# A new order for all instructions of a fused attention and feed-forward kernel, without the zero matmuls that followed the first transposes

## The chip, the core and the metric

The kernel runs on one core of a Trainium2 chip. A core has five engines with instruction streams of their own: TensorE (PE, matmuls into the eight PSUM banks), VectorE (DVE), ScalarE (ACT), GpSimd (POOL, which here issues the converting loads) and SyncE (SP, which issues stores and transposing DMAs). The streams are joined by semaphores only, so each engine runs its instructions in the order in which they were written. The metric is the device time of one execution in microseconds, as the median of several runs.

## What is computed

Attention with a local window of 96 positions and 8 global ones, 4 batches of 768 positions, 8 heads of 64, with a linear bias by distance; then a feed-forward layer, 512 to 2048 to 512, with a squared ReLU. Cut to what matters:

```python
scores = scale * np.matmul(q, k.transpose(0, 1, 3, 2)) + bias
scores = np.where(is_global | is_local, scores, -1000000000.0)
a = np.exp(scores - np.max(scores, axis=-1, keepdims=True))
a = a / (np.sum(a, axis=-1, keepdims=True) + 1e-09)
x = np.matmul(a, v)        # then (batch, position) x (head, dim) = 3072 x 512
h = x @ w_in
r = np.maximum(h, 0.0)
out = (r * r) @ w_out
```

## The kernel before

The 3072 positions are 24 tiles of 128, six to a batch. Two tiles make one block of the feed-forward layer, so there are 12 blocks.

**Attention of a tile j.** GpSimd loads q, k and v and converts them to bf16 (`ld.q.1` and so on, later `load.6`). For the first eight tiles TensorE transposes q and k (`tr.0.j` for q, `tr.1.j` for k), and VectorE or ScalarE copies the result out of its bank (`T.0.j`, `T.1.j`); from tile 8 on a DMA of SyncE does this (`T.8`). Tile 0 is loaded in fp32 by SyncE (`plain`). `sc.j` are the scores: the tile's queries against its own keys and those of the tile before, in four banks (two for the first tile of a batch). For the first three tiles the bias is put into the banks by matmuls (`bias.j`); later it is multiplied in after the exponential (`mul.j.g`, with tables E and, for the first tile of a batch, E0). `exp.j.odd.g` runs on ScalarE; the name has the odd or even heads and then the half. `pv.j.half` multiplies with v; `norm.j.half` divides by the sum (a reciprocal and a product on VectorE). The keys and values of the eight global positions are copied over rows that are no longer needed: `gk.j` and `gv.j`, which may run on VectorE, ScalarE or GpSimd (`kl.j` is a copy of the keys in a buffer of its own). `trx.j` transposes the result on TensorE, and `xT.j` copies it out; from tile 8 on `xT.j` is a DMA.

**Feed-forward.** Blocks 0 and 1 multiply plainly: `s1.blk.s` for one of 8 slices of the hidden dimension, `relu.blk.s` out of the bank, `sq.blk.s` to square it. From block 2 on the first product, and from block 1 on the second, is done with seven products in place of eight: `xs`, `sum`, `isum` and `wsum` are the sums and differences of the operands (VectorE), `h.blk.g.p1` to `p7` and `s2.blk.p1` to `p7` the products (TensorE), `u` and `part` copies of intermediate results out of a bank, `c` the combination of such a copy with a bank and the ReLU (one custom VectorE instruction, or a plain ReLU for c21), `q` the square, `o` the combination into the output tile, `st` its store.

**What sets the order.** Every step is an operation of a plan, and the string `ORDER` lists all of them in the order in which they are written out. After a `:` stand the PSUM banks that the step takes, after `@` the engine (A, V, P) where there is a choice; `#2` is the second operation of a name. The instructions of one engine stand in the order of this list; what one step waits for follows from the data, the banks and the buffers. Loads queue on GpSimd in the list's order, and a `gv@P` stands in the same queue.

**The start.** Before the plan begins, line 372 runs eight matmuls of zeros into bank 7, while nothing has landed yet. In the plan, `warm:7` (line 532) is eight more of them, between the transposes of the first q tile and those of the first k tile.

Of the kernel before, what the change touches and what calls it, by code (L numbers as in the profile page):

```python
# [62 lines left out]
T.1.4@V xT.1@V pv.2.1:0 ld.k.5 ld.win.2.0 exp.3.1.1 gk.3@A ld.win.2.1 norm.2.0 s1.0.3:2 mul.3.0 s1.0.6:4 ld.win.4.0
tr.0.4:7 ld.q.5 ld.v.4 norm.2.1 mul.3.1 relu.0.6@A s1.0.3#2 gv.2@P pv.3.0:3 norm.3.0 trx.2:5 T.0.4@A pv.3.1:6
ld.win.1.0 norm.3.1 ld.win.0.1 xT.2@A sc.4.0:1047 exp.4.1.1 exp.4.1.0 tr.1.5:3 T.1.5@A s1.0.2:5 trx.3:6 xT.3@V
ld.win.0.0 ld.win.5.0 s1.0.2#2 s1.0.2#3 s1.0.2#4 relu.0.3@V exp.4.0.1 ld.v.5 gv.3@P exp.4.0.0 gk.4@V sq.0.6@V
relu.0.2@A s1.1.3:7 ld.win.7.0 relu.1.3@A load.6 s1.1.6:0 mul.4.1 tr.0.5:6 mul.4.0 sq.0.3@V s1.1.2:3 T.0.5@A ld.wout.3
pv.4.0:2 ld.wout.1 sq.0.2@V sc.5.0:4157 ld.wout.0 s1.0.4:6 relu.1.2@A exp.5.1.1 s1.0.1:3 sq.1.3@A exp.5.0.0 relu.0.4@V
s1.1.4:7 ld.wout.2 norm.4.0 pv.4.1:4 gv.4@P norm.4.1 sq.0.4@A load.7 exp.5.1.0 sq.1.2@A relu.1.4@A s1.0.0:6 gate.9
ld.wout.4 mul.5.0 s1.0.0#2 sq.1.4@A s1.0.0#3 s1.1.5:2 trx.4:1 exp.5.0.1 relu.1.6@V s1.1.1:4 ld.wout.5 s1.0.1#2  # L70
relu.1.1@A E0.1 mul.5.1 relu.1.5@A pv.5.0:7 s1.1.7:0 s1.1.0:5 sq.1.1@V norm.5.0 ld.wout.6 E0.0 sq.1.5@V tr.1.6:4
sq.1.6@A pv.5.1:2 relu.1.7@A tr.0.6:7 s1.0.0#4 norm.5.1 xT.4@A sq.1.7@A h.2.0.p2:0 ld.wout.7 T.1.6@V h.2.1.p2:1
trx.5:2 xT.5@V relu.1.0@A sq.1.0@A gate.14 h.2.0.p1:5 xs.2.0 s1.0.5:4 sum.1.2 s1.0.7:2 relu.0.1@A xs.2.1 gate.10
sum.1.0 sum.1.1 relu.0.0@A T.0.6@A sc.6.0:36 wsum.0.0 sum.1.3 sq.0.0@A sq.0.1@A s2.0.0.0:7 relu.0.7@A s2.0.1.0 load.9
exp.6.0.0 xs.2.2 s2.0.2.0 exp.6.1.0 s2.0.3.0 s2.0.0.1:2 s2.0.1.1 wsum.2.0 relu.0.5@A sq.0.7@A s2.0.2.1 load.8 mul.6.0
wsum.1.0 s2.0.3.1 tr.0.7:3 tr.1.7:6 gate.15 isum.0.0 h.2.1.p1:4 T.0.7@A s2.0.4.0 isum.0.1 s2.1.p1.0:3 isum.3.1 T.1.7@A
sq.0.5@A pv.6.0:6 isum.1.1 s2.0.4.1 s2.0.5.1 u.2.0.1@A c.2.0.c11 s2.0.5.0 gate.11 u.2.1.1@A h.2.1.p6 q.2.0.c11@A
isum.1.0 T.8 s2.0.6.1 u.2.1.2@A s2.0.6.0 isum.3.0 pv.6.1:0 h.2.0.p6 wsum.2.1 wsum.0.1 s2.1.p1.1 s2.0.7.1 c.2.1.c11
norm.6.0 gate.13 o.0.1@V st.0.1 s2.0.7.0 h.2.1.p7 part.1.p1@A s2.1.p6.0 u.2.0.2@A o.0.0@A u.2.1.3@A h.2.0.p7 h.2.1.p4
T.9 norm.6.1 wsum.3.0 u.2.0.3@A sc.7.0:1762 c.2.1.c21@A wsum.1.1 h.2.1.p5:0 c.2.1.c22 q.2.1.c11@A s2.1.p2.0:4  # L80
exp.7.1.0 exp.7.0.0 isum.2.1 load.10 h.2.0.p4 exp.7.0.1 mul.7.0 exp.7.1.1 s2.1.p2.1 isum.2.0 s2.2.p1.0:7 q.2.1.c21@A
mul.7.1 h.2.0.p5:1 s2.1.p6.1 part.1.p6@A trx.6:6 gate.12 c.2.0.c21@A load.12 pv.7.0:2 xT.6@A c.2.0.c22 q.2.1.c22@A
q.2.0.c22@A s2.2.p1.1 h.2.1.p3 s2.1.p7.0 wsum.3.1 o.1.p2 norm.7.0 h.2.0.p3 pv.7.1:5 s2.1.p7.1 q.2.0.c21@A st.0.0
c.2.1.c12 s2.1.p5.0 s2.1.p5.1 part.1.p7@A q.2.1.c12@A s2.1.p4.0 T.10 s2.1.p4.1 c.2.0.c12 gk.7@V q.2.0.c12@A o.1.p5
o.1.p4@A sc.8.0:6201 st.1.1 part.2.p1@A s2.1.p3.0 norm.7.1 sum.2.0 sum.2.1 s2.1.p3.1 trx.7:5 xT.7@V o.1.p3 h.3.0.p1:3
exp.8.1.0 gk.8@V h.3.1.p1:2 exp.8.0.0 exp.8.1.1 exp.8.0.1 h.3.0.p2:6 xs.3.0 u.3.1.1@A sc.9.0:1540 s2.2.p6.0 mul.8.0
xs.3.1 mul.8.1 u.3.0.1@A h.3.0.p6 exp.9.0.1 exp.9.1.1 gv.7@V h.3.1.p2:4 c.3.0.c11 h.3.1.p6 c.3.1.c11 exp.9.0.0
pv.8.0:0 s2.2.p6.1 pv.8.1:6 load.11 norm.8.0 u.3.1.2@A s2.2.p2.0:1 sum.2.2 gv.8@P q.3.1.c11@A norm.8.1 xT.8 h.3.1.p7
h.3.0.p5:4 u.3.0.2@A h.3.0.p7 s2.2.p2.1 exp.9.1.0 st.1.0 part.2.p6@A xs.3.2 u.3.1.3@A q.3.0.c11@A h.3.1.p5:0 s2.2.p7.0
u.3.0.3@A mul.9.1 mul.9.0 s2.2.p7.1 c.3.1.c22 T.12 c.3.0.c22 pv.9.0:6 h.3.1.p3 o.2.p2 h.3.0.p4 c.3.1.c12 load.15  # L90
norm.9.0 q.3.1.c22@A h.3.0.p3 s2.3.p1.0:5 s2.3.p1.1 c.3.0.c12 q.3.0.c22@A pv.9.1:0 c.3.0.c21@A part.2.p7@A norm.9.1
q.3.1.c12@A h.3.1.p4 q.3.0.c12@A h.4.0.p1:3 c.3.1.c21@A s2.2.p5.0 part.3.p1@A gk.9@V sc.10.0:6402 s2.2.p5.1
q.3.0.c21@A sum.3.0 sum.3.1 s2.2.p4.0 s2.2.p4.1 exp.10.1.0 sum.2.3 exp.10.0.0 exp.10.0.1 h.4.0.p2:4 T.11 u.4.0.1@A
exp.10.1.1 gk.10@V gv.9@A s2.3.p6.0 o.2.p5 mul.10.0 c.4.0.c11 xT.9 h.4.1.p1:6 o.2.p4@A mul.10.1 s2.2.p3.0 s2.2.p3.1
q.3.1.c21@A s2.3.p2.0:0 sum.3.2 u.4.1.1@A pv.10.0:2 pv.10.1:4 s2.3.p6.1 xs.4.0 gate.17 o.2.p3 part.3.p6@A xs.4.1
s2.3.p2.1 norm.10.0 h.4.0.p6 h.4.1.p6 q.4.0.c11@A gv.10@A norm.10.1 u.4.0.2@A load.13 s2.3.p7.0 sc.11.0:7124 u.4.1.2@A
sum.3.3 h.4.0.p7 h.4.1.p7 xs.4.2 exp.11.1.0 o.3.p2 exp.11.0.0 u.4.0.3@V s2.3.p7.1 sc.12.0:17 exp.11.1.1 exp.11.0.1
# [67 lines left out]
def kernel(  # L165
# [119 lines left out]
    HALVES = ((NBLK - 2, 0), (NBLK - 2, 1))  # L285
# [176 lines left out]
    for j in range(NT):  # L462
# [127 lines left out]
        def emit_sc(e, gs, j=j, todo=todo, open_sc=open_sc):  # L590
# [4 lines left out]
            if j >= NBIAS:  # L595
                open_sc(gs)
# [835 lines left out]
```

## Time and profile before

| | us |
|---|---|
| median of 3 runs | 198.78 |
| the runs | 198.13, 198.78, 200.09 |
| the profiled execution | 199.37 |
| its span, first to last instruction | 197.6 |

A stage by stage look at the profile: the first loads land between 3.9 and 9 us; attention of the first tiles alone fills 8 to 18 us; from 18 us on the products of the feed-forward part run among the attention of later tiles; after 190 us only the last block's output is left. In a row of busy time by stretch, a number such as 8.25 (x156) is the busy time in us and the number of instructions. In a row of the groups, the columns are busy time, mean duration in ns of one instruction, idle time of the engine just before them, and what ended it. Neighbouring instructions of VectorE and ScalarE overlap a little, so a mean duration is a few per cent more than what one adds to the engine's busy time. Matmul durations overlap widely: there the distance from start to start counts, which the chain of waits shows.

### The profile page before, as it was taken

What the parts mean: (1) busy time and instruction counts of PE and PEld (TensorE: products, weight loads), DVE (VectorE), ACT (ScalarE), POOL (GpSimd) and SP (SyncE); (2) the same over time, 40 slices, a digit from 0 to 9 for tenths busy, and PEclk for the clock granted to TensorE, in tenths of its full rate; (3) what the DMA queues carried; (4) which work ended last, traced back from release to release, by engine and by line L of the source; (5) the groups of instructions that cost most, each with busy time, mean ns of one, the idle gap of its engine ahead of it and who ended that gap; (6) DMA issues with size and microseconds to landing.
All of it is one profiled execution on the core that took longest, in us unless ns stands there. A gap on an engine that the chain in (4) does not pass through costs nothing.

```text
span 197.6 us, 6777 instructions
## 1 busy us (share of the span) xinstructions
PE 191.9 (97%) x2776; PEld 169.6 (86%) x2776; DVE 173.2 (88%) x423; ACT 163.0 (82%) x335; POOL 80.4 (41%) x101
## 2 busy tenths in 40 slices
PE   7989999999999999999999999999999999999993
PEld 3578999866989999899989999989899989999992
DVE  8159869999999999799999999999899999989872
ACT  6379989966999898999789998998989879774750
POOL 8999988586045309603192903080410001000000
PEclk9999999999999999999999999999999999999999
DMA  6999999999999999999999999999695711114023
GB/s 127 153 158 171 181 181 185 182 202 159 139 209 191 75 200 88 145 174 210 151 129 203 114 124 194 160 121 92 136 81 116 154 55 56 27 30 163 0 106 106
DMA packets 111857, 26.91 MB, mean 136 GB/s; under 512 B 103379, under 2 KB 109011, under 8 KB 111827
## 3 DMA queue, kind: packets, MB, share of 16 engines
q0 software_dynamic: 80256, 13.37, 91.8%
q1 hardware_dynamic: 31570, 13.11, 32.5%
q8 instruction: 21, 0.34, 0.6%
q14 instruction: 10, 0.07, 0.1%
HBM read 27.26 MB, written 6.29 MB: 170 GB/s over the span
## 4 chain that ended last, share of the span: by engine, by line
PE 95%; DVE 2%; issue 1%; ACT 0%; DVEq 0%
PE bank L1212 35%; PE bank L950 32%; PE bank L1061 7%; PE bank L599 6%; PE bank L748 5%; PE bank L1339 4%; PE bank L372 2%; PE bank L506 2%; PE bank L532 1%; DVE qkT L433 1%; PE bank L816 1%; PE bank L579 0%; ACT qkT L429 0%; DVE o L1287 0%; DVE v L433 0%
## 5 line engine op out<-in xcount | busy, mean ns | idle before, releaser
L1015 ACT ACTIVATE hs<-hr 128x512 bf16<-128x512 f32 x72 | 44.8, 641 | 5.1 <-DVE hr L995 4.7
L665 ACT ACTIVATE esc<-bank 128x512 bf16<-128x512 f32 x78 | 42.9, 614 | 1.3 <-PE bank L599 1.0
L1212 PE MATMUL bank<-wsum,hsum 128*128 128x256 bf16 x264 | 36.2, 273 | 0.0
L1212 PEld LDWEIGHTS <-hsum 128*128 128x128 bf16 x360 | 32.1, 98 | 4.1 <-issue 0.5
L995 DVE CUSTOM_DVE_ANT_0 hr<-bank,early 128x512 f32<-128x512 f32 x45 | 30.4, 685 | 2.5 <-PE bank L950 1.5
L950 PEld LDWEIGHTS <-win 128*128 128x128 bf16 x480 | 29.7, 98 | 1.0
L950 PEld LDWEIGHTS <-qk_first 128*128 128x128 bf16 x480 | 29.7, 98 | 1.0
L429 ACT COPY early<-bank 128x512 f32<-128x512 f32 x42 | 24.5, 591 | 3.6 <-PE bank L950 3.3
L690 DVE TENSOR_TENSOR at<-esc,E 128x1024 bf16<-128x1024 bf16 x39 | 26.7, 696 | 0.1
L1212 PEld LDWEIGHTS <-hs 128*128 128x128 bf16 x264 | 24.0, 98 | 2.6
L310 POOL DMA_DIRECT2D qk<-in_q_dram x18 | 16.0, 890 | 21.9 <-DMA qkT<-qk 20.6
L1212 PE MATMUL bank<-wout,hs 128*128 128x256 bf16 x176 | 24.9, 273 | 0.0
L310 POOL DMA_DIRECT2D v<-in_v_dram x18 | 16.0, 888 | 18.3 <-DVE v L480 14.9
L950 PE MATMUL bank<-xT,win 128*128 128x128 bf16 x320 | 23.4, 219 | 0.0
L431 POOL COPY v<-v 8x520 bf16<-8x520 bf16 x8 | 5.7, 718 | 43.3 <-PE bank L748 43.3
L950 PE MATMUL bank<-xs,qk_first 128*128 128x128 bf16 x320 | 22.8, 219 | 0.0
L779 DVE TENSOR_TENSOR x<-bank,rs 128x256 bf16<-128x256 f32 x48 | 20.4, 425 | 1.7
L865 ACT ACTIVATE hr<-bank 128x512 f32<-128x512 f32 x33 | 19.4, 598 | 1.3 <-PE bank L950 0.4
L748 PE MATMUL bank<-v,at 128*128 128x65 bf16 x352 | 17.8, 193 | 0.0
L1287 DVE TENSOR_TENSOR o<-bank,part 128x256 f32<-128x256 f32 (+2 forms) x34 | 13.8, 410 | 3.3 <-PE bank L1212 3.2
L429 ACT COPY part<-bank 128x256 f32<-128x256 f32 x29 | 10.9, 375 | 7.1 <-PE bank L1212 6.9
L310 POOL DMA_DIRECT2D qk<-in_k_dram x18 | 16.1, 897 | 0.9 <-DMA win<-in_moe_w_in_dram 0.5
(92 smaller groups left out, 367.0 us busy)
## 6 DMA issues: line engine op xcount, KB each, us to landing
out_dram<-o SPq DMA_DIRECT2D x22, 256.0 KB, 2.5
v<-in_v_dram POOLq DMA_DIRECT2D x24, 128.0 KB, 5.6
qk<-in_q_dram POOLq DMA_DIRECT2D x18, 128.0 KB, 5.0
qk<-in_k_dram POOLq DMA_DIRECT2D x18, 128.0 KB, 5.8
wout<-in_moe_w_out_dram POOLq DMA_DIRECT2D x8, 256.0 KB, 8.5
win<-in_moe_w_in_dram POOLq DMA_DIRECT2D x6, 256.0 KB, 6.9
qk_first<-in_k_dram POOLq DMA_DIRECT2D x5, 128.0 KB, 5.6
qk_first<-in_q_dram POOLq DMA_DIRECT2D x5, 128.0 KB, 5.7
```

The source lines that it names most:

```text
L310: nc.gpsimd.dma_start(out=dst, in_=src)
L429: nc.scalar.copy(dst, src)
L665: nc.scalar.activation(out=tiles[tag, j, g][:, odd], in_=tiles.pop(("sc", j, odd, g)).rearrange("p a c -> p (a c)"), func=Act.Exp, scale=s ...
L690: nc.vector.tensor_mul(at, tiles.pop(("esc", j, g)), bias)
L748: nc.tensor.matmul(out=po[:, hi, :], lhsT=tiles["at", j, g][:, odd, at * P : (at + 1) * P], rhs=v_sb[kj][:, h, :], start=(i == 0), stop=(i ...
L779: nc.vector.tensor_tensor(out=x[:, 4 * hf : 4 * hf + 4, :], in0=po[:, :, :D], in1=rs.to_broadcast([P, 4, D]), op=Alu.mult,)
L865: nc.scalar.activation(dst, src, Act.Relu)
L950: nc.tensor.matmul(out=tiles["h", blk, g, bank][:, n], lhsT=left_[:, s, k], rhs=right_[:, k], start=opens and n == 0 and k == 0, stop=k == ...
L995: nc.vector._custom_dve(TENSOR_ADD_SAT, out=hr, in0=src, in1=tiles.pop(("u", blk, g, i)), s0=float("inf"), s1=0.0,)
L1015: nc.scalar.activation(hs, hr, Act.Square)
L1061: nc.tensor.matmul(out=hT[:, c, cols], lhsT=w_in_sb[s][:, kt, c * P : (c + 1) * P], rhs=tiles["xT", blk][:, kt, cols], start=(kt == 0), st ...
L1212: nc.tensor.matmul(out=tiles["acc", blk, bank][:, cols], lhsT=left_[:, s], rhs=right_[:, cols], start=first and s == 0, stop=s == NSTEP - ...
```

## The change

It replaces `ORDER` by another list: every step is there as before except `warm`, but in another order, with other banks and in part other engines. Two lines of the table show the form (the first of each; the rest says nothing to a reader):

```diff
-tr.0.0:0 warm:7 tr.1.0:1 T.1.0@V bias.0.0:23 T.0.0@A sc.0.0 ld.win.3.0 exp.0.0.0 ld.k.1 tr.1.1:4 bias.1.0:5670 T.1.1@V ld.q.1
...
+ld.q.1 ld.k.1 ld.v.0 ld.k.2 ld.q.2 ld.q.3 ld.v.1 ld.k.3 ld.q.4 ld.k.4 ld.v.2 ld.q.5 ld.k.5 ld.v.3 ld.win.3.0
...
-    NKEEP = 8
...
-        if j == 0:
-            def emit_warm(e):
-                for _ in range(NKEEP):
-                    nc.tensor.matmul(out=psum(), lhsT=zero[:, :P], rhs=zero, start=True, stop=True)
-
-            plan.op(("warm",), {"PE": 0.216 * NKEEP}, emit_warm, key=base)
...
-        def open_sc(gs, j=j):
-            for n, (g, odd) in enumerate((g, odd) for g in gs for odd in range(2)):
+        def open_sc(gs, at=0, j=j):
+            for n, (g, odd) in enumerate(((g, odd) for g in gs for odd in range(2)), at):
...
-                deps.append(glob.get(("v", j - 1)))
+                deps += [glob.get(("v", j - 1)), land["v", j - 1]]
...
-    u_next = [0]
+    u_free = list(u_ring)
...
-                    u = u_ring[u_next[0] % NU]
-                    u_next[0] += 1
+                    u = u_free.pop(0)
...
+                        u = tiles.pop(("u", blk, g, i))
+                        nc.vector._custom_dve(TENSOR_ADD_SAT, out=hr, in0=src, in1=u, s0=float("inf"), s1=0.0)
+                        u_free.append(u)
...
-                for o, cols in zip(done, cuts):
+                for o, cols in zip([done[-1]] * len(cuts), cuts):
```

Besides the table: the zero matmuls of line 532 go (those of line 372 stay); a buffer of `u` is taken from a list of free ones instead of in turn; `pv.j` also depends on the landing of the v tile before; and in the last block the two parts of `o.11.p3` depend on both parts of the last product, so that the bank is read once all of it is written. Three places show what the table does.

ScalarE, up to the first results of the feed-forward part. The first rows are of before: `esc` are exponentials of the scores (tile 3 here), `qkT` copies of transposed q and k, `hr` the ReLU of the first product, `s1.0.6`.

```order
L665 ACTIVATE at_317<-bank_0_107 128x512
L665 ACTIVATE esc_379<-bank_4_111 128x512
L665 ACTIVATE esc_379<-bank_3_110 128x512
L665 ACTIVATE esc_390<-bank_6_113 128x512
L665 ACTIVATE esc_390<-bank_1_108 128x512
L429 COPY qkT_3_84<-qkT_0_81 128x4x8
L865 ACTIVATE hr_441<-bank_4_111 128x512
```

And of the changed kernel, up to the exponentials of tile 4 (`esc_456`, `esc_471`) and the copies `xT.1` (`xT_320`, out of bank 4, which `sc.5.0` takes next) and `xT.2` (`xT_486`):

```order
L429 COPY qkT_4_85<-bank_2_109 128x512
L660 ACTIVATE esc_414<-bank_6_113 128x512
L660 ACTIVATE esc_456<-bank_2_109 128x512
L660 ACTIVATE esc_456<-bank_1_108 128x512
L660 ACTIVATE esc_471<-bank_0_107 128x512
L429 COPY xT_320<-bank_4_111 128x4x128
L429 COPY xT_486<-bank_1_108 128x4x128
L660 ACTIVATE esc_471<-bank_7_114 128x512
```

Before, ScalarE turned to the feed-forward part after the exponentials of tile 3; now those of tile 4 come first, and there is no `hr` yet. In TensorE's stream the first `s1` step, `s1.0.3`, stands behind `sc.5.0` now, where it stood behind `pv.2.1`.

VectorE, at the first results of the feed-forward part, before (`hs` is the square of `hr`, `at` the product of `esc` with the bias table, `rs` and `x` a `norm`):

```order
L867 TENSOR_SCALAR hr_532<-bank_2_109 128x512
L433 COPY qkT_4_85<-qkT_0_81 128x4x8
L1100 TENSOR_TENSOR hs_539<-hr_441 128x512
L690 TENSOR_TENSOR at_565<-esc_500,E_101 128x1024
L690 TENSOR_TENSOR at_571<-esc_502,E_101 128x1024
L1100 TENSOR_TENSOR hs_539<-hr_532 128x512
L1100 TENSOR_TENSOR hs_539<-hr_541 128x512
L867 TENSOR_SCALAR hr_635<-bank_6_113 128x512
```

and in the changed kernel:

```order
L685 TENSOR_TENSOR at_545<-esc_456,E_101 128x1024
L862 TENSOR_SCALAR hr_569<-bank_5_112 128x512
L773 RECIPROCAL rs_572<-bank_7_114 128x4
L774 TENSOR_TENSOR x_571<-bank_7_114,rs_572 128x256
L773 RECIPROCAL rs_575<-bank_1_108 128x4
L774 TENSOR_TENSOR x_571<-bank_1_108,rs_575 128x256
L862 TENSOR_SCALAR hr_602<-bank_6_113 128x512
L433 COPY xT_610<-bank_5_112 128x4x128
L862 TENSOR_SCALAR hr_631<-bank_7_114 128x512
L433 COPY v_4_75<-v_0_71 8x8x65
```

The ReLU out of the bank moved to VectorE for more steps, the squares to ScalarE, and copies of global values (`v_4`) from GpSimd and ScalarE to VectorE.

VectorE at the very end. Before and after read alike there, apart from numbers; what differs is what the row before the last waits for. In both, the last two rows are the two parts of `o.11.p3`, which read the same bank:

```order
L1281 TENSOR_TENSOR o_4100<-bank_6_113,part_4032 128x256
L1161 TENSOR_TENSOR hsum_4052<-hs_3870,hsum_4052 128x512
L1281 TENSOR_TENSOR o_4127<-bank_6_113,part_4112 128x256
L1281 TENSOR_TENSOR o_4100<-bank_6_113,part_4098 128x192
L1281 TENSOR_TENSOR o_4100<-bank_6_113,part_4098 128x64
```

The part of 192 columns used to be read between the two halves of the last product; now TensorE writes all 256 columns first.

More of the change, by code (lines that the diff above doesn't have):

```diff
@@ L63 @@
[L63 to L97, printed above, removed]
```

180 lines of the change are left out of this document (107 added, 73 removed).

## Prediction

> **What bounds the kernel now.** I read the page's busy shares and the chain that ended last, then busy time by stretch, because a share over the whole span mixes a thin start with a dense middle.
>
> ```profile
> PE 191.9 (97%) x2776; PEld 169.6 (86%) x2776; DVE 173.2 (88%) x423; ACT 163.0 (82%) x335; POOL 80.4 (41%) x101
> PE 95%; DVE 2%; issue 1%; ACT 0%; DVEq 0%
> ```
> ```profile
> 8.50:18.10 9.60, 8.25 (x156) 6.88 (x154) 6.14 (x22) 6.93 (x15) 9.60 (x12) 1.00 2.29 161
> ...
> 31.00:190.00 159.00, 159.00 (x2357) 143.39 (x2355) 149.92 (x346) 138.79 (x285) 51.34 (x61) 1.00 1.18 131
> ```
> ```profile
> 18.10:190.00 171.90, 171.90 (x2558) 155.20 (x2555) 160.33 (x372) 150.48 (x308) 63.13 (x77) 1.00 1.23 135
> ```
>
> The columns after the stretch's length are PE, PEld, DVE, ACT, POOL (busy us and instructions), clock, DMA. From 18.1 to 190 us TensorE is busy for 171.9 of 171.9 us. It runs the same matmuls after the change, so nothing can be won in there; a new order can only keep it or open gaps. What can be won lies in the first 18 us, where TensorE also waits or runs matmuls that nobody reads, and in the tail. How that start goes is shown by the chain and the timeline:
>
> ```profile
> 1.19 3.60 PE bank L372 x8
> 4.79 0.85 PE bank L506 x4
> 5.64 2.41 PE bank L532 x8
> 8.05 0.45 PE bank L506 x4
> ...
> 9.28 0.40 PE bank L599 x8
> ...
> 10.00 0.87 PE bank L579 x8
> ...
> 11.62 0.62 PE bank L599 x16
> ...
> 15.09 0.36 PE bank L748 x8
> ...
> 19.61 0.22 PE bank L506 x4
> ```
> ```profile
> 18.12 1.49 PE L1061 MATMUL bank<-xT,win 128*128 128x128 bf16 x16
> ```
>
> L532 are the removed zero matmuls. L1061 at 18.12 is the first product of the feed-forward part, `s1.0.3`; from there on TensorE is dense. So I ask of the new order: when does `s1.0.3` start, and how much more of TensorE's work is then behind it?
>
> **The sum goes against the profiled execution**, 199.37 us (span 197.6 and 1.77 around it); the median of the three runs, 198.78, lies 0.59 lower, and the result is given on the median's scale.
>
> **Term A, the start.** Ahead of `s1.0.3` the new order puts three more transposed loads (`tr`), two more score sets (`sc.4`, `sc.5`), two more halves of `pv` and one more `trx`. By the chain's rows: 4 x 0.22 + 2 x 0.62 + 2 x about 0.3 (0.36 with its wait) = 2.7 us. If `s1.0.3` starts at 18.1 + 2.7 = 20.8 us, nothing is won or lost. Its start hangs on ScalarE: `sc.5.0` takes bank 4, and that is read last by the copy `xT.1`, behind 17 exponentials. The rows for these:
>
> ```profile
> L665 ACT ACTIVATE esc<-bank 128x512 bf16<-128x512 f32 x78 | 42.9, 614 | 1.3 <-PE bank L599 1.0
> L429 ACT COPY qkT<-bank 128x512 bf16<-128x512 bf16 x7 | 4.0, 590 | 1.5 <-PE bank L506 1.5
> L429 ACT COPY qkT<-qkT 128x32 bf16<-128x32 bf16 x4 | 1.0, 240 | 0.0
> ```
> ```profile
> plain<-in_q_dram SPq DMA_DIRECT2D x1, 256.0 KB, 3.1
> plain<-in_k_dram SPq DMA_DIRECT2D x1, 256.0 KB, 6.0
> ```
> ```profile
> 1.25 0.56 SPq L319 DMA_DIRECT2D plain<-in_k_dram  x1
> 1.34 0.89 POOL L307 DMA_DIRECT2D win<-in_moe_w_in_dram  x1 [0.17 <-issue]
> ```
> ```profile
> win<-in_moe_w_in_dram POOLq DMA_DIRECT2D x6, 256.0 KB, 6.9
> ...
> qk_first<-in_q_dram POOLq DMA_DIRECT2D x5, 128.0 KB, 5.7
> ```
>
> 17 x 0.55 (42.9/78) + 5 copies x 0.59 + 2 x 0.24 = 12.8 us. It can start when the first k tile is there: 1.25 + 6.0 = 7.25 us, then its transposes (0.45 at full clock): 7.75. So the removed 2.41 us buy little: the chain has the transposes behind them at 8.05, and they can't begin before 7.25. ScalarE then waits twice, for `sc.0.0` (0.40 and a hop) and for `bias.1.0`, `tr.1.1`, `sc.1.0` less the two exponentials beside them (0.87 + 0.22 + 0.62 - 1.1): 1.1 us. 7.75 + 12.8 + 1.1 = 21.65, and `sc.5.0` itself 0.62: `s1.0.3` at 22.3, 1.5 late. Without any such wait it is 21.2, 0.4 late. Neighbouring exponentials also start closer than 0.55 where none waits, so I take +0.8. The upper end, +2.5, has both waits and a further one just behind: `pv.4.0` stands after `gv.3` on VectorE (0.44) and `pv.4.1` after `mul.4.1` (0.70), with little between. The lower end, -0.9, is the case in which the k tile lands with the q tile (rival 1). The loads don't set this: `win.3.0`, issued first before (1.34), now follows 14 loads of q, k and v. GpSimd issued 12 instructions in the 9.60 us of its stretch, 0.80 each: 1.34 + 14 x 0.80 + 6.9 = 19.4, in time.
>
> **Term B, the clock.** The page grants 1.0 throughout, yet the weight loads of L532 show when full speed really came:
>
> ```profile
> 5.86 0.15 PEld L532 LDWEIGHTS <-early 128*128 128x128 bf16 x1 [0.28 <-issue]
> 6.29 0.15 PEld L532 LDWEIGHTS <-early 128*128 128x128 bf16 x1 [0.28 <-issue]
> 6.71 0.15 PEld L532 LDWEIGHTS <-early 128*128 128x128 bf16 x1 [0.28 <-issue]
> 7.03 0.53 PEld L532 LDWEIGHTS <-early 128*128 128x128 bf16 x3 [0.16 <-issue]
> ```
>
> One each 0.43 us until 6.71, then three in 0.53: twice the speed, after 5.7 us of unbroken work since 1.19. Without L532 the work breaks off after the first transposes (at 4.79 + 0.85 = 5.64) and resumes at 7.25. If TensorE is then still at half speed, the transposes take 0.85 in place of 0.45, and `bias.0.0` (half the columns of the L579 row, so 0.44) with `tr.0.1` (0.22), now hidden under a copy of 0.59, take 1.3 and show 0.7; `sc.0.0` 0.2 more: +1.3 on the way to the first exponential, and up to 0.9 more if `bias.1.0` (0.87) is slow too. Ends: 0, if the clock rises as before, and +2.2. I take +1.0, as the break of 1.6 us follows only 4.45 us of work, less than the 5.7 that it took before. [...]
>
> **Term C, VectorE.** The new order moves evictions to VectorE. Net counts from the two tables: `relu` +6, `c` +2, `q` +2, `sq` -4, `gv` +4 (two from ScalarE, two from GpSimd), `o` +3, and T, part, u, kl, gk, xT near zero together.
>
> ```profile
> L867 DVE TENSOR_SCALAR hr<-bank 128x512 f32<-128x512 f32 x3 | 2.1, 685 | 1.3 <-PE bank L1061 1.3
> L1100 DVE TENSOR_TENSOR hs<-hr 128x512 bf16<-128x512 f32 x5 | 3.3, 684 | 0.1
> L1017 DVE TENSOR_TENSOR hs<-hr 128x512 bf16<-128x512 f32 x8 | 5.5, 686 | 0.1
> L433 DVE COPY v<-v 8x520 bf16<-8x520 bf16 x4 | 1.8, 438 | 0.0
> L1287 DVE TENSOR_TENSOR o<-bank,part 128x256 f32<-128x256 f32 x32 | 13.2, 418 | 2.1 <-PE bank L1212 2.0
> L779 DVE TENSOR_TENSOR x<-bank,rs 128x256 bf16<-128x256 f32 x48 | 20.4, 425 | 1.7
> L778 DVE RECIPROCAL rs<-bank 128x4 f32<-128x4 f32 x48 | 8.4, 175 | 2.2 <-PE bank L748 2.1
> L690 DVE TENSOR_TENSOR at<-esc,E 128x1024 bf16<-128x1024 bf16 x39 | 26.7, 696 | 0.1
> L433 DVE COPY qkT<-bank 128x512 bf16<-128x512 bf16 x7 | 2.9, 418 | 1.9 <-PE bank L506 1.9
> ```
>
> 8 x 0.685 + 2 x 0.686 - 4 x 0.684 + 4 x 0.438 + 3 x 0.418 = 7.1 us. Against that, more of VectorE's work is done ahead of `s1.0.3`: seven norms (0.175 + 0.425), eight copies (0.418), two `mul` (0.696), two `gv` (0.438) and the f32 copy of the first tile (as the L867 row, 0.685) are 10.5 us, where the stretch 8.5 to 18.1 shows 6.14: 4.4 more. So the dense stretch has 160.3 + 7.1 - 4.4 = 163.0 us of VectorE in 171.9 - 2.7 = 169.2 us of TensorE, where before it had 160.3 in 171.9. VectorE's slack falls from 11.6 to 6.2 us. If it needed all its old slack TensorE would wait 5.4; if the slack was only waiting for TensorE, none. ScalarE, at 138.79 of 159, gets lighter. I take +0.7, near the lower end, as TensorE never waited at 94%.
>
> **Term D, the tail.**
>
> ```profile
> 194.16 0.36 DVE L1287 TENSOR_TENSOR o<-bank,part 128x192 f32<-128x192 f32 x1 [0.84 <-PE bank L1212]
> 194.57 0.28 PE L1212 MATMUL bank<-wout,hsum 128*128 128x64 bf16 x4 [0.45 <-DVE o L1287]
> 194.88 0.22 DVE L1287 TENSOR_TENSOR o<-bank,part 128x64 f32<-128x64 f32 x1 [0.37 <-PE bank L1212]
> ```
>
> The last four matmuls waited 0.45 for a read of their bank. Now they run first and both reads follow: the last read ends at about 194.85 in place of 195.10. The larger store is then issued some 0.1 later, just ahead of the last. I take -0.1, ends -0.5 and +0.2.
>
> Sum: 0.8 + 1.0 + 0.7 - 0.1 = +2.4; 199.37 + 2.4 = 201.8, on the median's scale **201.2 us**. The new code's other edits (which of the four `u` buffers is free, one more dependency of `pv` on a landed v tile, bank offsets) add no instruction; the v tile had been read by the tile before, so that wait is over.
>
> **The rivals.**
>
> 1. Faster: the k tile lands early. Its 6.0 us against 3.1 for the q tile come with a weight load of 256 KB that GpSimd issues 0.09 us later; now a load of 128 KB is issued there. If k lands by 5.6, the transposes follow each other without a gap, the clock rises as before, and ScalarE starts 1.65 us sooner: `s1.0.3` at 21.2 - 1.65 = 19.6 if it never waits, 20.65 if it waits as above, so at best 1.2 ahead of 20.8, and with the loads' 19.4 as a floor. With the tail, another 0.5 from exponentials that start closer, and no term C: 198.78 - 1.8 = 197.0. It decides if k lands before 6. Against it: a load is still issued in that place, and the next ones 0.8 apart. [...] Chance 0.16.
> 2. No change: the start loses about 0.8 to 1.0 by A or B, and the head start of VectorE and ScalarE on the attention lets every short wait of TensorE go: 198.8 to 199.6. For it: TensorE has been kept dense at 94% VectorE. Chance 0.19.
> 3. VectorE becomes the bound: its slack can't fall, TensorE waits 5.4, and with A, B and D 198.78 + 7.1 = 205.9. It decides where VectorE needs more than 96% of a stretch. For it: 163.0 of 169.2 is 96%. Against: 159 us at 94% without one wait. Chance 0.12.
>
> My own case has 0.53 and spans 199.8 to 203.5.
>
> **How the numbers follow.** About 1% (2 us) is what a measurement of this kernel can tell from no change: its three runs lie 1% apart. Below 196.8 is half of rival 1: 0.08. Within 196.8 to 200.8: the other half, rival 2, and 0.18 of my case: 0.45. Above: 0.35 of my case and rival 3: 0.47. The range 197.3 to 204.4 leaves out some 0.10 below and 0.07 above.
>
> **What would show it.** A: `s1.0.3` after 21 us, and ScalarE without a gap from the second score set to `xT.1`. B: the first transposes of the k tile 0.21 apart, not 0.11, and bias matmuls of 256 columns 0.21 apart. C: waits of TensorE for VectorE after 31 us, above 1 us in all. D: no wait of L1212 before the last four matmuls. I am wrong if `s1.0.3` starts before 20.5 with the middle still dense (then faster), or if the waits of TensorE after 31 us exceed 4 us.

## The result and the profile after

| | before | after |
|---|---|---|
| median of all runs, us | 199.31 (198.13 to 200.88, 20 runs) | 201.35 (199.45 to 202.83, 20 runs) |
| the profiled execution, us | 199.37 | 201.37 |
| its span, us | 197.6 | 199.6 |

The ratio of after to before is 1.0087, with a 95% interval of 1.0059 to 1.0114: slower by 0.9%, inside the range of the prediction and 0.15 us beside its number. The ratio leaves out three slow runs of after (202.5 to 202.8 us), so it stands for 1.7 us where the medians differ by 2.0. Against before the forecast was +2.4 us, so the close hit of the time itself owes something to before, whose median rose from 198.78 to 199.31 with more runs. The two profiled executions differ by 2.0 us, as the medians do, so they can be compared term by term. That comparison shows that the number was right for other reasons than those given.

The page after has the busy time of the engines and the shares of the chain that ended last:

```profile
PE 191.5 (96%) x2765; PEld 168.7 (85%) x2768; DVE 178.4 (89%) x435; ACT 158.6 (79%) x325; POOL 79.2 (40%) x99
PE 80%; DVE 6%; POOL 5%; ACT 3%; DMA 3%; issue 2%; DVEq 0%; POOLq 0%
```

TensorE's share of the chain fell from 95% to 80%, and two names are new in it: POOL and DMA. VectorE does 5.2 us more than before; 7.1 were reckoned. Busy time by stretch of after, with the columns as before:

```profile
8.50:20.55 12.05, 9.80 (x192) 7.60 (x190) 9.19 (x29) 11.04 (x24) 12.05 (x15) 1.00 2.16 160
20.55:190.00 169.45, 168.20 (x2470) 150.78 (x2470) 159.52 (x367) 140.68 (x286) 59.48 (x72) 1.00 1.23 134
31.00:190.00 159.00, 157.80 (x2328) 141.49 (x2329) 150.66 (x345) 132.35 (x270) 50.54 (x60) 1.00 1.19 131
```

The middle is no longer dense: 1.2 us of TensorE's 159.00 are idle, where none was. The start, in the timeline and in the row of DMA issues (median us from issue to landing last):

```profile
4.58 1.91 PE L506 MATMUL bank<-ident,plain 128*128 128x128 f32 x8
6.29 0.83 PE L573 MATMUL bank<-pb,early 128*128 128x128 bf16 x8
...
7.84 1.04 PE L573 MATMUL bank<-pb,early 128*128 128x256 bf16 x8
...
20.55 1.07 PE L1055 MATMUL bank<-xT,win 128*128 128x128 bf16 x16
```
```profile
plain<-in_k_dram SPq DMA_DIRECT2D x1, 256.0 KB, 3.9
```

The k tile landed 3.9 us after its issue, not 6.0, so the eight transposes follow each other without a gap. They stand 0.21 us apart, where before the transposes of k stood 0.11 apart (from 7.89 us on): half that speed. The granted clock rose to 1.0 at 6.7 us, and the bias matmuls of 256 columns behind that, eight in 1.04 us, stand 0.11 us apart. `s1.0.3` starts at 20.55, where 20.8 was the point at which nothing is won or lost.

The chain of waits of that stretch (start, length, what) says what held the start instead:

```profile
7.62 2.53 POOL qk_first L307 x3
10.16 5.68 DMA v<-in_v_dram
15.83 0.04 issue
15.88 0.42 PE bank L743 x8
```

GpSimd's issuing of loads, one behind the other, then the landing of the v tile of tile 2, then the `pv` that reads it. TensorE itself waited 0.33 us for that landing; from 16.3 us on the chain runs through VectorE, up to a copy that ends at 20.00. At 77 us stands the one large wait of the middle (idle time before the row, and its releaser, in brackets):

```profile
71.55 1.20 SPq L835 DMA_TRANSPOSE xT<-x  x1
77.18 0.43 DVE L917 TENSOR_TENSOR xs<-xT 128x512 bf16<-128x512 bf16 x1 [1.03 <-DMA xT<-x]
77.99 0.62 PE L945 MATMUL bank<-xs,qk_first 128*128 128x128 bf16 x8 [0.81 <-ACT hs L1009]
```

TensorE's row names ScalarE's `hs`, but `xs` is formed by VectorE at 77.18, and VectorE had been idle for 1.03 us until a transposing DMA landed. That is the true releaser. The tail:

```profile
195.16 1.06 PE L1206 MATMUL bank<-wout,hsum 128*128 128x192 bf16 x16
195.40 0.37 ACT L429 COPY o<-bank 128x256 f32<-128x256 f32 x1 [1.42 <-PE bank L1206]
196.25 0.49 DVE L1281 TENSOR_TENSOR o<-bank,part 128x192 f32<-128x192 f32 x2 [1.28 <-PE bank L1206]
```

The wait of 0.45 us is gone. From the start of the last product to the end of the span it is 199.6 - 195.16 = 4.4 us; before it was 197.6 - 193.18 = 4.4 as well.

### The profile page after: what moved, and what is told of

Same layout as the page of the kernel before. It is cut to its first block, busy times and chain, and to the rows that moved or that the text cites. A ratio compares the mean times of both kernels' runs of the same rounds, so it can differ in the third digit from the quotient of the medians.

```text
span 199.6 us, 6754 instructions
## 1 busy us (share of the span) xinstructions
PE 191.5 (96%) x2765; PEld 168.7 (85%) x2768; DVE 178.4 (89%) x435; ACT 158.6 (79%) x325; POOL 79.2 (40%) x99
## 4 chain that ended last, share of the span: by engine, by line
PE 80%; DVE 6%; POOL 5%; ACT 3%; DMA 3%; issue 2%; DVEq 0%; POOLq 0%
PE bank L1206 30%; PE bank L945 30%; PE bank L1055 7%; PE bank L743 4%; PE bank L594 4%; POOL qk_first L307 4%; PE bank L1333 3%; DMA v<-in_v_dram 3%; DVE at L685 2%; ACT hs L1009 1%; POOL v L307 1%; ACT esc L660 1%; DVE hr L990 1%; DVE x L774 1%; DVE hsum L1161 1%
## 5 line engine op out<-in xcount | busy, mean ns | idle before, releaser
L1009 ACT ACTIVATE hs<-hr 128x512 bf16<-128x512 f32 x70 | 43.4, 643 | 3.9 <-DVE hr L990 3.5
L660 ACT ACTIVATE esc<-bank 128x512 bf16<-128x512 f32 x78 | 43.6, 609 | 2.4 <-PE bank L594 2.2
L990 DVE CUSTOM_DVE_ANT_0 hr<-bank,early 128x512 f32<-128x512 f32 x46 | 31.3, 683 | 1.0 <-ACT hs L1009 0.4
L429 ACT COPY early<-bank 128x512 f32<-128x512 f32 x43 | 25.2, 593 | 8.5 <-PE bank L945 7.0
L1206 PE MATMUL bank<-wout,hs 128*128 128x256 bf16 x176 | 25.4, 273 | 0.0
L945 PE MATMUL bank<-xs,qk_first 128*128 128x128 bf16 x320 | 24.3, 219 | 0.9 <-ACT hs L1009 0.8
L310 POOL DMA_DIRECT2D v<-in_v_dram x18 | 16.3, 904 | 14.4 <-DVE v L480 9.2
L860 ACT ACTIVATE hr<-bank 128x512 f32<-128x512 f32 x25 | 14.9, 602 | 3.4 <-PE bank L945 2.4
L743 PEld LDWEIGHTS <-at 128*128 128x128 bf16 x352 | 15.1, 98 | 2.7 <-DVE at L685 1.4
L1055 PE MATMUL bank<-xT,win 128*128 128x256 bf16 (+1 forms) x160 | 15.9, 251 | 0.1
```

Of the source, the lines that this page charges most:

```text
L310: nc.gpsimd.dma_start(out=dst, in_=src)
L429: nc.scalar.copy(dst, src)
L660: nc.scalar.activation(out=tiles[tag, j, g][:, odd], in_=tiles.pop(("sc", j, odd, g)).rearrange("p a c -> p (a c)"), func=Act.Exp, scale=s ...
L743: nc.tensor.matmul(out=po[:, hi, :], lhsT=tiles["at", j, g][:, odd, at * P : (at + 1) * P], rhs=v_sb[kj][:, h, :], start=(i == 0), stop=(i ...
L860: nc.scalar.activation(dst, src, Act.Relu)
L945: nc.tensor.matmul(out=tiles["h", blk, g, bank][:, n], lhsT=left_[:, s, k], rhs=right_[:, k], start=opens and n == 0 and k == 0, stop=k == ...
```

## The experiments

All ratios are to the kernel before, with 95% intervals, five rounds each. For several runs a table gives the *lead* of TensorE: the start of a matmul in the reference kernel less the start of the same matmul in the run, in us, worked out from the two traces by matching TensorE's matmuls in order. A lead that stays level is kept; where it drops, something else than TensorE's own work came last. Each lead comes from one profile of each kernel. How far such profiles differ by themselves is seen from e6, e7, e9, e10 and e11, which run the same instructions as the changed kernel up to 77 us: `s1.0.3` starts at 20.54, 20.94, 19.65, 20.53 and 19.65 there.

**e1: before without the zeros.**

```diff
-tr.0.0:0 warm:7 tr.1.0:1
+tr.0.0:0 tr.1.0:1
```

> The kernel before without the eight zero matmuls of its plan (they feed no result); everything else as it was, the 256 KB weight load still first on GpSimd. Theory 1 (term B of the prediction, the clock falls back in the gap): the k tile lands at about 7.2 us as before, TensorE is idle from 5.6 to 7.2, and its transposes, the bias matmuls and the first scores then run at half speed (transposes 0.21 us apart): ratio to before 1.000 to 1.010. Theory 2 (the clock rises about 7 us after the start whatever stands in the gap, as the trace after the change suggests, where no gap arose): transposes 0.11 apart or 0.21 only for the first ones, the chain starts some 0.3 us earlier, ratio 0.995 to 1.000.

Ratio 1.0027 (0.9996 to 1.0057): no difference that can be told. It lies in theory 1's range, but theory 1's premise, a gap up to 7.2 us, did not occur: with the 256 KB weight load still first, the k tile landed 4.2 us after its issue, at 5.47.

**e2: before with the q tile loaded first.**

```diff
-ld.win.3.0 exp.0.0.0 ld.k.1 tr.1.1:4 bias.1.0:5670 T.1.1@V ld.q.1
+ld.q.1 exp.0.0.0 ld.k.1 tr.1.1:4 bias.1.0:5670 T.1.1@V
...
-ld.q.2 tr.0.2:3
+ld.q.2 ld.win.3.0 tr.0.2:3
```

> The kernel before with one load moved: the 128 KB q tile is issued first on GpSimd, the 256 KB piece of the weights that stood there comes after the q tile 2 load. Zeros stay. Theory (rival 1's mechanism: the first load of GpSimd decides when the k tile of SyncE lands): k lands 3.9 to 4.2 us after its issue in place of 6.0. The zeros keep TensorE until 8.05, so the time stays: ratio 0.997 to 1.003. Rival (the k tile lands early in the changed kernel for another reason): k lands 5.5 to 6.0 us after its issue, same ratio.

Ratio 0.9991 (0.9959 to 1.0022). k landed after 4.0 us, which looks like the theory, but e1 had 4.2 without the edit. So the first load of GpSimd does not decide it.

**e3: both.**

> The kernel before with both: the q tile first on GpSimd, and no zero matmuls. Theory 1 (the start is worth what rival 1 said, and the changed kernel lost it again by its own order between 10 and 20 us): the second score set comes about 2 us sooner, the first product of the feed-forward part at 16.3 to 17.0 us in place of 18.1, ratio 0.988 to 0.995, so faster than both kernels. Theory 2 (the lead is lost on later landings and on ScalarE in any order, as in the changed kernel): the first product of the feed-forward part at 17.5 to 18.2, ratio 0.997 to 1.002.

Ratio 1.0009 (0.9983 to 1.0035), although `s1.0.3` started at 16.09, 2.0 us sooner than before and sooner than theory 1 had it. TensorE still waits 0.9 us for copies of VectorE (1.1 before). The largest of its other waits are for loads and, at 90 us, for a transposing DMA:

```profile
11.10 0.40 PE L506 MATMUL bank<-ident,qk_first 128*128 128x128 bf16 x4 [0.78 <-DMA qk_first<-in_k_dram]
...
14.49 0.40 PE L506 MATMUL bank<-ident,qk_first 128*128 128x128 bf16 x4 [0.31 <-DMA qk_first<-in_k_dram]
...
89.99 0.23 PE L593 MATMUL bank<-qkT 64*128 64x128 bf16 x2 [0.68 <-DMA qkT<-qk]
```

**e12: e3 with two more loads reordered.**

```diff
-ld.q.2 ld.win.3.0 tr.0.2:3 norm.0.0 ld.k.2 T.0.2@V ld.k.3
+ld.q.2 tr.0.2:3 norm.0.0 ld.k.2 T.0.2@V ld.k.3 ld.win.3.0
...
-ld.win.6.0 sc.3.0:4361 ld.q.4 norm.1.1 ld.v.3
+ld.v.3 ld.win.6.0 sc.3.0:4361 ld.q.4 norm.1.1
```

> The kernel before without the zero matmuls and with the 128 KB q tile first on GpSimd, as in the run e3, and two more loads reordered: the first 256 KB piece of the weights now follows the k tiles 2 and 3, and the v tile 3 comes ahead of the second piece. Theory 1 (the landing of k, k and v tiles ends TensorE's waits of 0.78, 0.31 and 0.39 us at 10 to 19 us in the run e3, so the order of loads sets the start, and a lead is then kept by the order before, whose middle hardly waits): TensorE is 1.6 to 2.4 us ahead of the kernel before at 30 us (1.1 in e3), ratio 0.990 to 0.996, faster than both kernels. Rival (transposing DMAs and loads take the lead back between 80 and 110 us, as 0.96 us of e3's were): the lead at 30 us is there, but under 0.6 us is left at 110 us; ratio 0.997 to 1.002.

Ratio 1.0017 (0.9993 to 1.0041). Theory 1 fell, even in its first half: the waits for the k tiles 2 and 3 went, and three others stood up for what had been moved back. The ratio lies in the rival's range, but by luck, as the lead that the rival expected at 30 us was not there either (0.21).

```profile
13.82 0.40 PE L742 MATMUL bank<-v,at 128*128 128x65 bf16 x8 [1.22 <-DMA v<-in_v_dram]
15.43 0.40 PE L506 MATMUL bank<-ident,qk_first 128*128 128x128 bf16 x4 [0.46 <-DMA qk_first<-in_k_dram]
18.47 1.05 PE L1055 MATMUL bank<-xT,win 128*128 128x256 bf16 x8 [0.82 <-DMA win<-in_moe_w_in_dram]
```

TensorE's lead over the kernel before, at times of that kernel:

| us | 9.3 | 17.4 | 21.5 | 29.5 | 41.7 | 78 | 98 | 110 | 191 |
|---|---|---|---|---|---|---|---|---|---|
| e1 no zeros | 1.97 | 1.32 | 1.21 | 1.13 | 0.19 | 0.44 | 0.44 | -0.09 | -0.09 |
| e2 q first | 0.62 | 0.57 | 0.78 | 0.73 | 0.55 | 0.60 | 0.60 | 0.60 | 0.60 |
| e3 both | 2.50 | 1.83 | 1.15 | 1.09 | 0.91 | 1.13 | 0.39 | 0.17 | 0.17 |
| e12 loads | 2.49 | 0.89 | 0.21 | 0.21 | 0.25 | 0.27 | 0.13 | -0.86 | -0.86 |

Two things take most of a lead of 2 us. Up to 35 us it is the loads (in e1 one of these waits, 0.34 us, stands at 33.9): GpSimd issues one each 0.87 us, and in e1, e3 and e12 alike some tile came late. After 80 us it is transposing DMAs (`qkT<-qk` at 90 in e3, `xT<-x` ahead of the drop between 98 and 110 in e1 and e3).

**e4: after with the weight load first.**

```diff
-ld.q.1 ld.k.1 ld.v.0 ld.k.2 ld.q.2 ld.q.3 ld.v.1 ld.k.3 ld.q.4 ld.k.4 ld.v.2 ld.q.5 ld.k.5 ld.v.3 ld.win.3.0
+ld.win.3.0 ld.q.1 ld.k.1 ld.v.0 ld.k.2 ld.q.2 ld.q.3 ld.v.1 ld.k.3 ld.q.4 ld.k.4 ld.v.2 ld.q.5 ld.k.5 ld.v.3
```

> The changed kernel with the 256 KB piece of the weights first on GpSimd again, as before the change. Theory 1 (the prediction's own case hung on the k tile landing at 7.25; with this it happens): k lands at 7.0 to 7.3 us, the transposes of the k tile stand behind a gap, the first product of the feed-forward part starts at 21.5 to 22.5 us in place of 20.55, ratio to the kernel before 1.014 to 1.020. Theory 2 (the waits between 12 and 20 us come from other things and absorb the late start): it starts at 20.5 to 21.0, ratio 1.007 to 1.011.

Ratio 1.0180 (1.0148 to 1.0213), `s1.0.3` at 22.30: theory 1's numbers by another cause. k landed at 5.10. But every other load came later, and TensorE waited for the first of them:

```profile
8.17 0.40 PE L506 MATMUL bank<-ident,qk_first 128*128 128x128 bf16 x4 [1.45 <-DMA qk_first<-in_q_dram]
8.50 0.40 PE L594 MATMUL bank<-qkT 64*128 64x128 bf16 x8
9.02 0.40 PE L506 MATMUL bank<-ident,qk_first 128*128 128x128 bf16 x4
9.25 1.04 PE L573 MATMUL bank<-pb,early 128*128 128x256 bf16 x8
```

The matmuls behind this gap of 1.45 us ran at full speed (eight of 256 columns in 1.04 us). It is nearly as long as the gap that term B had (1.6 us), but it stands elsewhere: the granted clock had risen at 5.9 us, ahead of it, while term B's gap was to come before the rise.

**e5: after with the zeros put back.**

```diff
-T.0.0@V tr.1.0:1
+T.0.0@V warm:7 tr.1.0:1
```

> The changed kernel with the eight zero matmuls put back between the transposes of the first q and k tile. Theory 1 (the start is held by the loads, which GpSimd issues 0.87 us apart, and by what follows them, so that most of a lead or a lag of TensorE at 6 us is gone at 20 us): the first product of the feed-forward part starts at 20.6 to 21.6 us (20.55 without zeros), ratio to the kernel before 1.009 to 1.014. Rival (the chain from TensorE through ScalarE sets it, as terms A and B of the prediction had it): 22.0 to 22.6 us, ratio 1.016 to 1.020.

Ratio 1.0190 (1.0146 to 1.0233), `s1.0.3` at 21.40, later than in any of the six profiles that share the order without zeros. By its place the first theory, by its time the rival; in the profiled execution (span 200.8) the end came 1.2 us later than in the changed kernel. So the two don't agree on the size. In this order zeros cost something between 1.2 and 2 us, in the order before they cost nothing.

**e6: after with the tail as before.**

```diff
-s2.11.p3.0#2 s2.11.p3.1#2 o.11.p3 st.11.0#2
+s2.11.p3.0#2 o.11.p3 s2.11.p3.1#2 st.11.0#2
...
-                for o, cols in zip([done[-1]] * len(cuts), cuts):
+                for o, cols in zip(done, cuts):
```

> The changed kernel with the tail as before: the 192 columns are read between the two halves of the last product, and stored in that place. From the start of the last product to the end of the span it was 4.42 us before and 4.44 after. Theory (term D is nothing: the 0.54 us wait is traded against reads and stores that start later): 4.38 to 4.46 us, ratio to before 1.007 to 1.010. Rival (the later reads and stores cost, and the wait was hidden by the stores): 3.9 to 4.2 us, ratio 1.004 to 1.007.

Ratio 1.0097 (1.0064 to 1.0131), and from the start of the last product (195.48) to the end of the span (199.9) 4.4 us: the tail edit is worth nothing either way.

**e8: after with a table built later.**

```diff
-xT.0@V E0.1 sc.2.0
+xT.0@V sc.2.0
...
-mul.5.0 E0.0 T.0.6@V
+mul.5.0 E0.0 E0.1 T.0.6@V
```

> The changed kernel with one table for the first tile of a batch (a copy and a maximum, 0.9 us on VectorE) built at 28 us, where VectorE stood idle for 0.86 us, in place of 12.5 us, ahead of a norm and of the copy for which TensorE waits 0.93 us at 13.4. Theory 1 (VectorE's order costs in the start, the share of term C that lies ahead of the dense stretch): the wait at 13.4 falls to 0.1 to 0.4 us and the first product of the feed-forward part starts 0.3 to 0.7 us sooner (19.9 to 20.25), ratio to before 1.005 to 1.007. Rival (the landing of a v tile at 15.8 us holds the rest): the wait moves to 15.3 us, the first product starts at 20.4 to 20.6, ratio 1.008 to 1.010.

Ratio 1.0091 (1.0054 to 1.0129): the rival, one tile further on than I had it. The wait at 13.4 fell from 0.93 to 0.42, TensorE was 0.97 us ahead of the changed kernel at 16.3, and then the v tile of tile 3 landed 6.2 us after its issue at 12.75, that is at 18.9. In the changed kernel, which issues its loads in the same order, it landed at 18.0:

```profile
v<-in_v_dram POOLq DMA_DIRECT2D x1, 128.0 KB, 6.2
```
```profile
19.03 0.40 PE L743 MATMUL bank<-v,at 128*128 128x65 bf16 x8 [1.46 <-DVE qkT L433]
```

The `pv` of this row reads that tile, so it could not start before 18.9; the copy of VectorE that the row names ended 0.1 us after the landing. The lead at 21.3 us was -0.07. How late this tile lands differs between executions of one order, so the trace shows what took the lead in this execution. For all ten the ratio shows only that no gain was left.

**e7 and e9: the wait at 77 us.** Both put other work ahead of it on VectorE and TensorE; e9's edit (e7 leaves `o.2.p3` where it was):

```diff
-gv.10@V xs.4.0 xs.4.1 h.4.1.p6 o.2.p3
+gv.10@V norm.10.1 o.2.p3 xs.4.0 xs.4.1 s2.3.p2.1 sc.11.0:4276 h.4.1.p6
```

> The changed kernel with three steps moved ahead of the place where TensorE waited 0.81 us at 77 us (VectorE waits there for the transposing DMA of tile 9 before it can form xs of block 4): a norm of tile 10 on VectorE, and on TensorE the second half of a product of block 3 and the scores of tile 11 (some 0.9 us of work). Theory 1 (this wait is on the path that sets the end): the wait falls below 0.3 us, ratio to before 1.003 to 1.006. Rival (the next transposing DMA or VectorE takes it back at 90 to 110 us): the wait goes, and a wait of 0.4 us or more stands later that was not there; ratio 1.007 to 1.010.

> The changed kernel with the place at 77 us rearranged: VectorE does the second norm of tile 10 and reads the last bank of block 2 before it waits for the transposing DMA of tile 9, and TensorE does half a product of block 3 and the scores of tile 11 (0.9 us of work) before the product that needs xs of block 4. Theory 1 (the wait of 0.81 us for that DMA is on the path that sets the end): it falls below 0.3 us and TensorE is 0.5 to 0.9 us ahead of the changed kernel after it, ratio to before 1.003 to 1.006. Rival (the next transposing DMA, at about 93 us, takes it back): the lead is gone again before 110 us, with a wait of 0.4 us or more that was not there; ratio 1.007 to 1.010.

In e7 the scores of tile 11 overwrite two banks before block 2's last output is read from them, so part of the output is wrong; its ratio was 1.0138 (1.0107 to 1.0168). e9 had 1.0144 (1.0111 to 1.0177): not faster than the changed kernel, and by intervals that just touch slower. The wait itself went: TensorE's lead over the changed kernel rose from 0.86 to 1.85 us by 82 (the 0.86 it had from the start, ahead of the edit). It was taken back at the next places, and by more than the rival said: 1.13 at 87, 0.07 at 97, -0.70 at 107. One of these is the next block's transposing DMA:

```profile
91.98 0.43 DVE L917 TENSOR_TENSOR xs<-xT 128x512 bf16<-128x512 bf16 x1 [1.32 <-DMA xT<-x]
...
93.27 0.61 PE L945 MATMUL bank<-xs,qk_first 128*128 128x128 bf16 x8 [0.90 <-DVE xs L917]
```

**e10 and e11: VectorE relieved, alone and with e9's edit.**

```diff
-kl.15@V c.5.1.c21@V o.4.p4@V gv.13@V gv.15@V part.5.p7@V q.6.1.c12@V u.5.1.2@V
+kl.15@A c.5.1.c21@A o.4.p4@A gv.13@P gv.15@P part.5.p7@A q.6.1.c12@A u.5.1.2@A
```

> The changed kernel with eight steps between 85 and 145 us taken from VectorE (5 us of its work: two copies of global values to GpSimd; a copy of keys, a ReLU, a square and three copies out of banks to ScalarE, three of which the kernel before also had there). Theory C (VectorE's load is what the middle lost): the waits of TensorE for VectorE at 103, 105.5, 146 and 151 us (0.13, 0.29, 0.29 and 0.16 us beyond their pace) fall to under 0.3 us in all, TensorE is 0.5 to 0.9 us ahead of the changed kernel at the end, ratio to before 1.003 to 1.006. Rival (they come from the order, not the load, or ScalarE becomes late): at most 0.3 us ahead, or waits for ScalarE in their place; ratio 1.007 to 1.010.

> The two edits before this one together. Theory (the middle's waits are two separate things, a DMA at 77 us and VectorE from 103 to 151 us, and make up most of the 2 us that the changed kernel lost): 1.2 to 1.8 us less than the changed kernel, ratio to before 0.999 to 1.003. Rival (what is gained is lost to other landings): ratio 1.005 to 1.010.

Both were far outside every expectation: 1.0574 (1.0523 to 1.0625) and 1.0609 (1.0563 to 1.0654), some 10 us slower than the changed kernel. What TensorE waited for after 31 us in e10 (us in total, times, longest):

```profile
PE bank L743 <- POOL v L431: 4.1, 1, 4.1
PE bank L945 <- ACT early L429: 1.5, 1, 1.5
PE bank L945 <- ACT u L429: 0.8, 1, 0.8
PE bank L945 <- ACT o L429: 0.7, 1, 0.7
PE bank L743 <- ACT o L429: 0.6, 1, 0.6
```

A copy of global values (`gv.13`) moved to GpSimd stood behind five loads there, the first of which had itself waited until 99.45 us for a transposing DMA. The copies moved to ScalarE came late too, each for a bank that TensorE wanted. A second price came on top: 1.0 us after TensorE had resumed from the standstill of 4.1 us, the granted clock fell to 0.5 and stayed there for 3.41 us (from 105.47 to 108.88; matmuls of 256 columns 0.213 us apart in place of 0.109), which is 1.7 us more. In e11 the same followed a standstill of 2.8 us. So the price of the edit was where the moved steps now stood in their queues, and the ratio says nothing about VectorE's load. Two of the waits do: the changed kernel loses 0.29 us at 146.8 and 0.18 at 151.8 beyond the median distance of such matmuls, and e10 and e11 lose 0.29 and 0.18 at the same matmuls, with 5 us less work on VectorE ahead of them. Those two come from the order there, as the rival had it, not from the load.

## Why the prediction was right in its number and wrong in its steps

**Term A (+0.8 expected), with rival 1.** The step that failed is "it can start when the first k tile is there: 1.25 + 6.0 = 7.25", and with it rival 1's "a weight load of 256 KB that GpSimd issues 0.09 us later". The 6.0 was the median of a group of one. The trace of before has the landing in 16 parts: fifteen were there by 4.87 us, the sixteenth at 7.25. In the thirteen other profiles of this study the last part came between 5.10 and 5.63, with the weight load first (e1, e4) or not. Rival 1's condition, k before 6 us, therefore held, and so did its start with ScalarE's waits (20.65). Its result, 197.0, did not come, as it had no loss behind the start. ScalarE's chain was sized well: its copies and 17 exponentials ran from 6.53 to 19.74, 13.2 us where 12.8 + 1.1 were reckoned, and from 9.46 on it stood idle once, for 0.21 us. But it did not come last. `sc.5.0` waited for a copy of VectorE that ended 0.26 us later, at 20.00, and its chain leads back to a v tile and to GpSimd, which term A names as harmless: "The loads don't set this". The floor worked out there was for one weight tile; the attention tiles ahead of it have a floor each. e4 shows what they are worth: k landed early, the other loads came later, and `s1.0.3` came 1.75 us later. `s1.0.3` at 20.55 means -0.25 by the break-even of 20.8. The head start of TensorE at 6 to 9 us was real and was spent waiting for v tiles and for VectorE's and ScalarE's copies between 12.9 and 20 us.

**Term B (+1.0 expected): no gap, so not as forecast.** Half of its sign came all the same: the transposes of k stood 0.21 us apart, because the clock rose only at 6.7 us. In e9 and e7, the same order up to there with the rise at 4.3 and 4.5, TensorE was 0.64 and 0.71 us ahead at the first scores; at `s1.0.3` e9 was still 0.9 ahead and e7 0.39 behind. So what a late rise costs at `s1.0.3` stays open. It is contained in the -0.25 above, and it differs between executions of one order. Whether a gap ahead of the rise puts it off, as term B had it by the author's estimate, no run shows: e4's 1.45 us gap, which did not lower the clock, came after the rise. Nor did the zeros raise it sooner. Full speed was first reached between 4.1 and 7.0 us in fourteen profiles, at 7.0 in before with zeros, at 5.7 in e5 with zeros and at 4.5 in e3 without. Near-identical starts (first matmul at 1.2 us) reach it 2.9 to 5.8 us later, so the 5.7 us of work that the prediction read from before stand at the late end of a spread. By the granted clock the rise came before 5.64 us, where term B's gap was to begin, in seven of the fourteen profiles.

**Term C (+0.7 expected): about +2.0, the term that was mis-sized, and in part of another kind.** Behind 31 us the changed kernel lost 1.2 us of TensorE's busy time; overlapping durations hide the rest, so it has to be counted from start to start. Ahead of `s1.0.3` the new order has 16 more matmuls of 128 columns for `tr` and `trx` (0.056 us apart), two more sets of scores (0.55 us each) and 16 more matmuls for `pv` (0.49 us in all): 2.5 us, not the 2.7 taken from single durations. From `s1.0.3` to the start of the last product it was 193.18 - 18.12 = 175.06 us before and 195.16 - 20.55 = 174.61 after, with 2.5 less to do: 2.05 lost. Some 0.8 to 1.0 of it is the wait at 77 us, which is no lack of VectorE: it ends with a transposing DMA. The rest stands in distances between matmuls that are 0.1 to 0.3 us longer than the median for the same pair, mostly at 22, 40 to 46, 146 and 152 us. The transposing DMA of tile 9 took 2.5 us before and 5.6 after:

```profile
xT<-x SPq DMA_TRANSPOSE x1, 2.5
```
```profile
xT<-x SPq DMA_TRANSPOSE x1, 5.6
```

Busy time of before and then of after in the two stretches of 2 us around it; the last two columns are the DMA share and GB/s:

```profile
72.00:74.00 2.00, 2.00 (x37) 1.63 (x35) 1.93 (x6) 2.00 (x5) 0.00 (x0) 1.00 1.14 165
74.00:76.00 2.00, 2.00 (x26) 1.85 (x24) 1.79 (x5) 2.00 (x5) 1.71 (x2) 1.00 0.29 54
```
```profile
72.00:74.00 2.00, 2.00 (x30) 1.89 (x27) 1.73 (x5) 2.00 (x6) 0.98 (x3) 1.00 1.94 170
74.00:76.00 2.00, 2.00 (x38) 1.75 (x36) 1.87 (x5) 1.68 (x5) 1.76 (x2) 1.00 1.94 158
```

Before, GpSimd issued no load between these two:

```profile
66.69 0.88 POOL L310 DMA_DIRECT2D v<-in_v_dram  x1
74.29 0.87 POOL L310 DMA_DIRECT2D qk<-in_q_dram  x1 [6.73 <-DMA qkT<-qk]
```

In the new order it issues six between 67.6 and 74.0 us, and from 70 to 76 us the DMA share is 2.27, 1.94 and 1.94 by stretches of 2 us, where before it was 1.49, 1.14 and 0.29. The prediction counted the instructions that the table moved on VectorE and never asked which loads now stand beside which transposing DMA. The rows have the two side by side: 2.5 us beside a DMA share of 1.14 and 0.29, 5.6 beside 1.94. Over all `xT` transfers of both kernels, the four with about four loads in flight on average took 4.9 to 5.6 us, and the ten with under 0.4 took 2.4 to 4.2. Loads are not all of it, since one with 0.5 loads but two other transposing DMAs beside it took 5.0. And three of the long ones are of before, where TensorE waited for none: the length costs only where `xs` is needed soon.

**Term D (-0.1 expected): 0**, by 4.4 us from the last product to the end in before, after and e6. What the wait had cost went into the later reads and stores; how it splits between them was not separated.

Together, with the break-even at 20.6 by the 2.5 us: the start (A and B) about -0.1, C +2.05, D 0, which is the 2.0 us between the two profiles. Forecast were +1.8, +0.7 and -0.1. That the sum came out near is luck: the start was put 1.9 too high and the dense stretch 1.35 too low. **Rival 3** was wrong: VectorE is busy for 150.66 of the 159 us and did not become the bound. **Rival 2** expected the head start of VectorE and ScalarE to take TensorE's short waits away; the middle got new ones instead.

**What stays open.** Whether the wait at 77 us would go for good if the loads were spread as before was not tried; e9 only moved work into it. What VectorE's load does to the smaller waits at 103 to 106 us was not separated from the rest, and the longer distances at 22 and 40 to 46 us were not traced to a cause. That e9's loss after 82 us is due to transposing DMAs is shown for the one at 92, and for the others not. And no version beat the kernel before: e2, e3 and e12 are the nearest, and all three intervals hold 1.

## What to carry to other kernels

An engine that is 97% busy, as TensorE was, can still be paced by a queue that runs beside it: before pricing a head start, list for each of its next steps the landing of the tile it reads, because a head start ends at the first that is late (e12's lead of 2.49 us at 9.3 us was 0.21 at 21.5), and do the same for the copies of the other engines. When an order moves loads, lay them beside every other transfer of the same time, and when a step is moved to an idle engine, price what stands ahead of it in that engine's queue, not the engine's idle time. And a row that is the median of a single transfer is one draw: look at its parts before a start time is built on it.

## What the hardware showed that was not expected

- One of sixteen parts of a transfer can come late by itself: 4.87 us for the fifteenth and 7.25 for the last, once in fourteen profiles.
- The clock's rise moves by 2.9 us (4.1 to 7.0) between executions that start alike, and a gap of 1.45 us shortly after it (e4) does not undo it. Standstills of 4.1 us (e10) and 2.8 us (e11) in the middle were followed, 1.0 and 0.6 us after work resumed, by 3.41 us at a granted clock of 0.5.
- The transposing DMA of tile 9 took 2.5 us in one order and 5.6 in the other; with four converting loads in flight such transfers took 4.9 to 5.6 us, with hardly any 2.4 to 4.2.
- GpSimd's loads of 128 KB are issued 0.87 us apart. In e8 they landed 4.5 to 4.7 us after their issue until the v tile issued at 12.75, which took 6.2; of those issued behind it up to 19.2 us none took less. The longer time, once there, stayed.
